# Merging score visits across batch borders in an attention plus MLP kernel

## The chip, the cores and the metric

The kernel runs on one core of one Trainium2 chip. The metric is the device time of one execution in microseconds. Executions are compared by their medians, and ratios are the mean time of one kernel's fast runs over that of the other's of the same rounds, so not quite the ratio of the medians quoted beside them.

## The reference

```python
# B, H, S, Nb, D = 8, 8, 576, 16, 64;  d_model 512, d_ff 2048
k_all = concat([beacon_k, k], axis=2);  v_all = concat([beacon_v, v], axis=2)
scores = q @ k_all.T / sqrt(D), causal over the S keys, free over the Nb beacon keys
a = softmax(scores);  attn = a @ v_all
x = attn.transpose(0, 2, 1, 3).reshape(B * S, H * D)        # 4608 x 512
out = relu(x @ w_in) ** 2 @ w_out
```

## The kernel before

The kernel does not issue its work in program order. It builds a list of operations, each with engines, an assumed duration, a priority and what it needs. A small list scheduler (`Order.run`) plays them against its own clock and emits each engine's instructions in the order that falls out. One added or removed operation therefore shifts the order of everything behind it, and no line of a diff shows that.

The four pairs of heads of a batch give 4 x 1664 = 6656 score columns, that is 13 pieces of 512. The scores contract over 64 rows, so TensorE runs them on half-height tiles, two heads side by side, while all its other work in the stretch that matters here uses the full array. Pieces are therefore gathered in visits of two or three:

```python
PLAN = ((2,2,3,3,3),(2,2,3,3,3),(2,3,3,3,2),(2,3,3,3,2),(2,3,3,3,2),(2,3,3,3,2),(2,3,3,3,2))
...
def add_batch(b):
    ...
    for size in PLAN[b - 1]:
        pos = HP * b + 512.0 * n / PW
        runs = [(0,), (1, 2)] if size == 3 else [tuple(range(size))]
        for k, run in enumerate(runs):
            ...
            qk = add(f"qk{b}.{n + run[0]}", "PE", ..., emit,
                     take=None if k else ("strip", "strip", min(size, 2)),   # two-bank strips, 2 exist
                     gate=None if k else gate_at(pos - SHIFT))               # paced by MLP progress
            if k == 0:
                qk.wide = [None] if size == 3 else []                        # a third piece: 2 of 4 single banks
```

After a visit ScalarE exponentiates each piece (L632 for a strip, L674 for one head of a piece in single banks), VectorE masks it (L715, L719), and TensorE multiplies it with v (L741). The MLP (L904, then L942) fills TensorE in between. The queue of SyncE holds loads, the DMA transposes of q and k (L407) and of the attention output (L791, into `xT`), and the stores.

The softmax here doesn't subtract the row's maximum and nothing guards it: scores larger than these inputs give would overflow.

Of the kernel before, what the change touches and what calls it, by code (L numbers as in the profile page):

```python
# [11 lines left out]
AF = mybir.ActivationFunctionType  # L12
# [35 lines left out]
class Order:  # L48
# [16 lines left out]
    def add(self, *a, **kw):  # L65
        op = Op(*a, **kw)
        op.need = [d for d in op.need if d is not None]
        self.ops.append(op)
        return op
# [134 lines left out]
def kernel(  # L204
# [11 lines left out]
    nc = tc.nc  # L216
    B, H, S, D = q.shape
    Nb = beacon_k.shape[2]
    HP = H // 2
    scale = 1.0 / float(D) ** 0.5  # L220
# [13 lines left out]
    def sb(name, shape, dt):  # L234
        return pool.tile(shape, dt, name=name)

    NSTG, RB = 8, 4
    PW = 1664
# [34 lines left out]
    pt = sb("pt", [128, 2, 8192], BF16)  # L273
# [8 lines left out]
    strips = [psum.tile([128, 2, 512], FP32, name=f"strip{i}") for i in range(2)]  # L282
    ps = [psum.tile([128, 512], FP32, name=f"ps{i}") for i in range(4)]
# [16 lines left out]
    add = order.add  # L300
# [33 lines left out]
    qk_ops = {}  # L334
    av_ops = {}
    load_chain = []

    def t_rows(t):
        return 128 - Nb if t == 0 else rows_of(t)

    def t_start(t):
        return max(0, 128 * t - Nb)
# [207 lines left out]
    class Phase:  # L550
# [3 lines left out]
        def __init__(self, pieces, diag, last, tiles, off):  # L554
            self.pieces, self.diag, self.last, self.tiles, self.off = pieces, diag, last, tiles, off
            self.lo = t_start(tiles[0])
            self.hi = t_start(tiles[-1]) + t_rows(tiles[-1])
# [7 lines left out]
    NPC = HP * PW // 512  # L565
    PIECES = [[] for _ in range(NPC)]
    WHOLE = []
    for pr, segs in enumerate(STREAM):
        off, at = {}, 0
        for c, t0, t1 in segs:  # L570
# [3 lines left out]
            while t0 < t1:  # L574
                n, o = divmod(PW * pr + at, 512)
                w = min(t1 - t0, 512 - o)
                PIECES[n].append((pr, c, t0, t0 + w, o))
                t0, at = t0 + w, at + w
# [31 lines left out]
    def gate_at(pos):  # L610
        return lambda o: o.progress >= mlp_chunk_us * (LEAD + PACE * (pos - HP))

    def deps_of(b, pr, part):
        if b >= NPE:
            return trans[b, "k"] + trans[b, "q"]
        parts = range(part + 1) if b == pr == 0 else [len(parts_of[b]) - 1]
        return [bk_ev[b]] + [trans_part[b, n, pr, x] for n in parts for x in "kq"]

    def emit_scores(b, mms, st):
        for pr, c, t0, t1, at in mms:  # L620
            for hj in range(2):
                hp = slice(64 * hj, 64 * hj + 64)
                nc.tensor.matmul(  # L623
                    st[hj][:, at:at + t1 - t0],
                    kT[b % 2][hp, pr, 128 * c:128 * c + 128],
                    qT[b % 2][hp, pr, t0:t1],
                    start=True, stop=True,
                )

    def add_exp(name, qk, s, at, width, prio, done):  # L630
        def emit(e):
            nc.scalar.activation(pt[:, :, at:at + width], strips[qk.slots[s]][:, :, 0:width],  # L632
                                 AF.Exp, bias=0.0, scale=scale)

        return add(name, "ACT", 0.18 + 2 * width / 1200.0, emit, prio=prio, deps=[done], give=(qk, s))

    exps_of = {}
    SHIFT = 0.25
    PLAN = ((2,2,3,3,3),(2,2,3,3,3),(2,3,3,3,2),(2,3,3,3,2),(2,3,3,3,2),(2,3,3,3,2),(2,3,3,3,2))
    FREE = 2  # L640
    last_qk = []

    def add_batch(b):
        for pr in range(HP):
            p = HP * b + pr
            qk_ops[p], av_ops[p], exps_of[p] = [], [], []
        n = 0
        for size in PLAN[b - 1]:
            pos = HP * b + 512.0 * n / PW
            box = {}  # L650
            runs = [(0,), (1, 2)] if size == 3 else [tuple(range(size))]
            for k, run in enumerate(runs):
                def emit(e, run=run, n=n, box=box, size=size):
                    for s in run:
                        if size == 3 and s == 0:
                            emit_scores(b, PIECES[n], [ps[x] for x in box["qk"].wide])
                        else:
                            st = strips[box["qk"].slots[s - (size == 3)]]
                            emit_scores(b, PIECES[n + s], [st[:, 0, :], st[:, 1, :]])

                qk = add(f"qk{b}.{n + run[0]}", "PE", 0.2 / len(runs) + 512 * len(run) / 2400.0, emit,
                         prio=-1.0e6 if k else 100.0 * pos - 1000.0, behind=[qk] if k else last_qk[-1:] if size == 3 or b > FREE else [],
                         take=None if k else ("strip", "strip", min(size, 2)), gate=None if k else gate_at(pos - SHIFT))
                last_qk.append(qk)
                if k == 0:
                    qk.wide = [None] if size == 3 else []
                    box["qk"] = qk
                for s in run:
                    at, prio = 512 * (n + s), 1.0e-2 * (pos + 0.1 * s) - 30.0
                    if size == 3 and s == 0:  # L670
                        es = []
                        for hj in range(2):
                            def emit_half(e, hj=hj, at=at, qk=qk):
                                nc.scalar.activation(pt[:, hj, at:at + 512], ps[qk.wide[hj]], AF.Exp, bias=0.0, scale=scale)  # L674

                            es.append(add(f"exp{b}.{n}.{hj}", "ACT", 0.18 + 512 / 1200.0, emit_half, prio=prio + 1.0e-4 * hj, deps=[qk],
                                          give=(qk, hj - 2)))
                    else:
                        es = [add_exp(f"exp{b}.{n + s}", box["qk"], s - (size == 3), at, 512, prio, qk)]
                    for pr in sorted({mm[0] for mm in PIECES[n + s]}):  # L680
                        p = HP * b + pr
                        for o in deps_of(b, pr, 0) + av_ops[p - HP]:
                            if o not in box["qk"].need:
                                box["qk"].need.append(o)
                        qk_ops[p].append(qk)
                        exps_of[p] += es
            n += size
        assert n == NPC
        for pr in range(HP):
            add_phase(b, pr, HP * b + pr, 0, WHOLE[pr][0], 100.0 * (HP * b + pr), exps_of[HP * b + pr])  # L690

# [290 lines left out]
    for b in range(B):  # L982
# [8 lines left out]
        for n, (x, c) in enumerate(([] if b < NPE else nat) + [("v", c) for c in range(NT)]):  # L991
            behind, sync = [], []
            if x == "v" and b == 0:
                pass
            elif x == "v" and b == 1 and c == 0:
                behind = [strided[1, 0, HP - 1, "q"]]
            elif b == 2 and n == 0:
                sync = [w_ops["out", 2]]
            elif b >= NPE and x == "v" and c == 0:
                for y in "qk":  # L1000
                    add_trans(b, y, lp - 5.0)
                behind = trans[b, "q"] + trans[b, "k"]
# [7 lines left out]
        if b == 0:  # L1010
            for pr in range(HP):
                add_pair(b, pr)
        else:
            add_batch(b)
# [63 lines left out]
```

## Time and profile before

| | before |
|---|---|
| time, median of 3 | 338.86 us (338.78 to 339.68) |
| span of the profiled execution | 336.1 us, of a run that took 337.79 us |
| TensorE busy | 98% |
| VectorE, ScalarE, GpSimd busy | 50%, 57%, 27% |
| score visits in batches 4 to 7 | 20 |

TensorE is the bound, and a busy share cannot say how much of it is work. Throughout, the times are read from one start to the next: a matmul's listed length overlaps its neighbour, its start does not. Where a start comes later than the columns of the previous matmul explain, at 2.4 columns per ns plus some 2.5 ns, TensorE was switching or waiting. The other thing to know is that some matmul records are lost: the page before counts 3158 matmuls where the program has 3201 (its 3201 weight loads are all listed). A hole of 0.21 to 0.22 us beside 512-column matmuls is such a record and no wait.

### The profile page before, as it was taken

What the parts mean: (1) busy time and instruction counts of PE and PEld (TensorE: products, weight loads), DVE (VectorE), ACT (ScalarE), POOL (GpSimd) and SP (SyncE); (2) the same over time, 40 slices, a digit from 0 to 9 for tenths busy, and PEclk for the clock granted to TensorE, in tenths of its full rate; (3) what the DMA queues carried; (4) which work ended last, traced back from release to release, by engine and by line L of the source; (5) the groups of instructions that cost most, each with busy time, mean ns of one, the idle gap of its engine ahead of it and who ended that gap; (6) DMA issues with size and microseconds to landing.
All of it is one profiled execution on the core that took longest, in us unless ns stands there. A gap on an engine that the chain in (4) does not pass through costs nothing.

```text
span 336.1 us, 7810 instructions
## 1 busy us (share of the span) xinstructions
PE 329.0 (98%) x3158; PEld 189.0 (56%) x3201; DVE 168.4 (50%) x393; ACT 191.3 (57%) x289; POOL 90.9 (27%) x143
## 2 busy tenths in 40 slices
PE   8999999999999999999999999999999999999996
PEld 7577766445564554555458845554555544444444
DVE  4896995058556971477155823674247302301400
ACT  3877865376468736575747674676457216515621
POOL 9684805126306413150334042403000000000000
PEclk9999999999999999999999999999999999999999
DMA  7999999999999997899899989996210231011003
GB/s 139 226 205 219 205 194 213 213 235 212 160 241 224 195 197 137 220 242 182 143 230 226 199 154 177 216 238 126 72 62 2 46 90 62 0 64 62 0 3 125
DMA packets 143955, 51.74 MB, mean 154 GB/s; under 512 B 130702, under 2 KB 138798, under 8 KB 143918
## 3 DMA queue, kind: packets, MB, share of 16 engines
q1 hardware_dynamic: 135375, 42.19, 60.9%
q0 software_dynamic: 7904, 8.69, 15.0%
q8 instruction: 25, 0.41, 0.5%
q10 hardware_dynamic: 639, 0.36, 0.4%
q14 instruction: 12, 0.10, 0.1%
HBM read 37.22 MB, written 9.44 MB: 139 GB/s over the span
## 4 chain that ended last, share of the span: by engine, by line
PE 94%; POOL 2%; DMA 2%; issue 1%; ACT 0%; POOLq 0%; ACTq 0%
PE ps L904 37%; PE ps L942 36%; PE ps L741 9%; PE strip L623 6%; PE ps L623 2%; DMA qk_area<-in_k_dram 2%; PE ps L808 1%; PE ps L487 1%; PE ps L854 1%; POOL qk_area L452 1%; PE ps L296 1%; POOL stg L372 1%; POOL tri L312 0%; ACT osb L326 0%; POOL stg L371 0%
## 5 line engine op out<-in xcount | busy, mean ns | idle before, releaser
L904 PE MATMUL ps<-xT,w_in 128*128 128x512 bf16 (+3 forms) x686 | 132.1, 339 | 0.8
L942 PE MATMUL ps<-w_out,g 128*128 128x512 bf16 x535 | 127.0, 379 | 1.7 <-issue 0.5
L904 PEld LDWEIGHTS <-w_in 128*128 128x128 bf16 x704 | 65.5, 98 | 51.0 <-issue 0.7
L920 ACT ACTIVATE g<-ps 128x512 bf16<-128x512 f32 (+2 forms) x112 | 63.9, 570 | 41.9 <-PE ps L904 40.7
L632 ACT ACTIVATE pt<-strip 128x1024 bf16<-128x1024 f32 (+3 forms) x86 | 81.5, 1004 | 9.0 <-PE strip L623 8.8
L929 DVE TENSOR_TENSOR g<-g 128x1024 bf16<-128x1024 bf16 (+2 forms) x80 | 52.5, 666 | 65.8 <-ACT g L920 64.8
L942 PEld LDWEIGHTS <-g 128*128 128x128 bf16 x560 | 51.6, 98 | 56.5 <-issue 1.5
L328 POOL CAST qk_area<-stg 128x512 bf16<-128x512 f32 (+2 forms) x60 | 40.3, 675 | 65.5 <-DMA stg<-in_k_dram 39.9
L326 ACT COPY osb<-ps 128x512 f32<-128x512 f32 (+2 forms) x34 | 19.3, 571 | 64.6 <-PE ps L942 50.9
L741 PEld LDWEIGHTS <-pt 128*128 128x128 bf16 (+1 forms) x960 | 36.4, 98 | 11.7 <-DVE pt L715 0.8
L328 POOL CAST vb<-stg 128x512 bf16<-128x512 f32 (+1 forms) x38 | 24.4, 651 | 68.5 <-DMA stg<-in_v_dram 66.2
L741 PE MATMUL ps<-vb,pt 128*128 128x65 bf16 (+1 forms) x960 | 39.5, 194 | 0.0
L715 DVE TENSOR_TENSOR pt<-pt,tri 128x512 bf16<-128x512 bf16 x64 | 28.7, 457 | 17.9 <-ACT pt L674 11.3
L922 DVE TENSOR_SCALAR g<-ps 128x512 bf16<-128x512 f32 (+2 forms) x48 | 27.3, 586 | 13.5 <-PE ps L904 11.8
L760 DVE TENSOR_TENSOR xn<-ps,rcp 128x320 bf16<-128x320 f32 (+2 forms) x64 | 31.5, 492 | 2.5 <-DVE rcp L758 0.2
L674 ACT ACTIVATE pt<-ps 128x512 bf16<-128x512 f32 x42 | 22.8, 597 | 15.4 <-PE ps L623 13.1
L758 DVE RECIPROCAL rcp<-ps 128x5 f32<-128x5 f32 (+2 forms) x64 | 12.2, 190 | 33.0 <-PE ps L741 30.0
L623 PEld LDWEIGHTS <-kT 64*128 64x128 bf16 x596 | 19.8, 94 | 15.2 <-issue 13.3
L623 PE MATMUL strip<-qT,kT 64*128 64x208 bf16 (+13 forms) x474 | 27.0, 239 | 0.0
L328 DVE COPY osb<-ps 128x512 f32<-128x512 f32 (+1 forms) x4 | 2.4, 592 | 21.3 <-PE ps L854 11.7
L296 PE MATMUL ps<-g 128*128 128x128 bf16 (+1 forms) x87 | 11.0, 281 | 1.1 <-DVE warm L303 1.1
L372 POOL DMA_DIRECT2D stg<-in_v_dram x10 | 8.6, 866 | 4.5 <-DMA w_in<-in_moe_w_in_dram 3.0
(43 smaller groups left out, 98.2 us busy)
## 6 DMA issues: line engine op xcount, KB each, us to landing
out_dram<-osb SPq DMA_DIRECT2D x17, 512.0 KB, 3.5
stg<-in_q_dram SPq DMA_DIRECT2D x24, 256.0 KB, 5.0
stg<-in_k_dram SPq DMA_DIRECT2D x18, 256.0 KB, 5.5
stg<-in_v_dram SPq DMA_DIRECT2D x18, 256.0 KB, 5.2
w_in<-in_moe_w_in_dram POOLq DMA_DIRECT2D x4, 512.0 KB, 8.3
w_out<-in_moe_w_out_dram POOLq DMA_DIRECT2D x4, 512.0 KB, 11.2
stg<-in_v_dram POOLq DMA_DIRECT2D x6, 256.0 KB, 7.9
stg<-in_k_dram SPq DMA_DIRECT2D x6, 224.0 KB, 3.7
```

The source lines that it names most:

```text
L328: eng[e].tensor_copy(dst, src)
L623: nc.tensor.matmul(st[hj][:, at:at + t1 - t0], kT[b % 2][hp, pr, 128 * c:128 * c + 128], qT[b % 2][hp, pr, t0:t1], start=True, stop=True,)
L632: nc.scalar.activation(pt[:, :, at:at + width], strips[qk.slots[s]][:, :, 0:width], AF.Exp, bias=0.0, scale=scale)
L674: nc.scalar.activation(pt[:, hj, at:at + 512], ps[qk.wide[hj]], AF.Exp, bias=0.0, scale=scale)
L715: nc.vector.tensor_tensor(out=d, in0=d, in1=tri[:, m0:m0 + m, :][:, None].to_broadcast([128, 2, m, 128]), op=ALU.min)
L741: nc.tensor.matmul(a[:, at + (t - tl[0]) * (D + 1):at + (t - tl[0] + 1) * (D + 1)], P[0:rr, hj, o:o + 128], vb[b % 2][0:rr, c, 2 * pr + hj ...
L760: nc.vector.tensor_tensor(out=xn[b % 2].rearrange("p t (h d) -> p h t d", d=D)[:, h0:h0 + nh, tl[0]:tl[0] + nt], in0=a[:, :, :, 0:D], in1= ...
L904: nc.tensor.matmul(h[:, lo - spans[0][0]:hi - spans[0][0]], w_in_sb[:, mc, ft * 128:(ft + 1) * 128], xT[:, mc, lo % RING:lo % RING + hi - lo],
L920: nc.scalar.activation(dst, h, AF.Relu, bias=0.0, scale=1.0)
L922: nc.vector.tensor_scalar(out=dst, in0=h, scalar1=0.0, scalar2=None, op0=ALU.max)
L929: nc.vector.tensor_tensor(out=d, in0=d, in1=d, op=ALU.mult)
L942: nc.tensor.matmul(o, G[:, fc, ts * 128:(ts + 1) * 128], w_out_sb[:, fc, :], start=(fc == 0), stop=(fc == NFT - 1))
```

## The change

The intent is fewer visits. A batch of 13 pieces needs five visits of at most three; four batches together have 52 pieces, which fit into 18 visits where four times five are 20. The plan becomes one list over all batches, and a visit may take its last pieces from the next batch.

```diff
-    PLAN = ((2,2,3,3,3),(2,2,3,3,3),(2,3,3,3,2),(2,3,3,3,2),(2,3,3,3,2),(2,3,3,3,2),(2,3,3,3,2))
+    sizes = list((2,2,3,3,3, 2,2,3,3,3, 2,3,3,3,2, 3,3,3,3,3,3,3,3,3,3,3,3,3,3,3,3,2,2))
+    class Visit:                     # holds its ops and (batch, piece) parts; emits scores of both batches
+        ...
+        for n in range(NPC):
+            if not opened:
+                opened.append(Visit(b, n, sizes.pop(0)))
+            opened[0].add(b, n)
+            if len(opened[0].parts) == opened[0].size:
+                opened.clear()
-        for size in PLAN[b - 1]:
-            ...                      # the same, visit by visit within one batch
```

The title given to the change also names zeroing of batch 0 on VectorE. No line of the diff does that.

More of the change, by code (lines that the diff above doesn't have):

```diff
@@ L638, with __init__, emit, banks @@
     SHIFT = 0.25
-    PLAN = ((2,2,3,3,3),(2,2,3,3,3),(2,3,3,3,2),(2,3,3,3,2),(2,3,3,3,2),(2,3,3,3,2),(2,3,3,3,2))
     FREE = 2
-    last_qk = []
+    sizes = list((2,2,3,3,3, 2,2,3,3,3, 2,3,3,3,2, 3,3,3,3,3,3,3,3,3,3,3,3,3,3,3,3,2,2))
+    assert sum(sizes) == NPC * (B - 1)
+    last_qk, opened = [], []
+    class Visit:
+        def __init__(self, b, n, size):
+            pos = HP * b + 512.0 * n / PW
+            self.size, self.parts, self.ops = size, [], []
+            for k, run in enumerate([(0,), (1, 2)] if size == 3 else [tuple(range(size))]):
+                def emit(e, run=run):
+                    for s in run:
+                        bb, m = self.parts[s]
+                        emit_scores(bb, PIECES[m], self.banks(s))
+                self.ops.append(add(
+                    f"qk{b}.{n + run[0]}", "PE", (0.1 if size == 3 else 0.2) + 512 * len(run) / 2400.0, emit,
+                    prio=-1.0e6 if k else 100.0 * pos - 1000.0,
+                    behind=self.ops[-1:] if k else last_qk[-1:] if size == 3 or b > FREE else [],
+                    take=None if k else ("strip", "strip", min(size, 2)), gate=None if k else gate_at(pos - SHIFT)))
+            self.ops[0].wide = [None] if size == 3 else []
+            last_qk.append(self.ops[-1])
+        def banks(self, s):
+            first = self.ops[0]
+            if self.size == 3 and s == 0:
+                return [ps[x] for x in first.wide]
+            st = strips[first.slots[s - (self.size == 3)]]
+            return [st[:, 0, :], st[:, 1, :]]
+        def add(self, b, n):
+            s = len(self.parts)
+            self.parts.append((b, n))
+            first, op = self.ops[0], self.ops[-1 if s else 0]
+            at, prio = 512 * n, 1.0e-2 * (HP * b + 512.0 * n / PW) - 30.0
+            if self.size == 3 and s == 0:
+                es = []
+                for hj in range(2):
+                    def emit_half(e, hj=hj):
+                        nc.scalar.activation(pt[:, hj, at:at + 512], ps[first.wide[hj]], AF.Exp, bias=0.0, scale=scale)
+                    es.append(add(f"exp{b}.{n}.{hj}", "ACT", 0.18 + 512 / 1200.0, emit_half, prio=prio + 1.0e-4 * hj,
+                                  deps=[op], give=(first, hj - 2)))
+            else:
+                es = [add_exp(f"exp{b}.{n}", first, s - (self.size == 3), at, 512, prio, op)]
+            for pr in sorted({mm[0] for mm in PIECES[n]}):
+                p = HP * b + pr
+                for o in deps_of(b, pr, 0) + av_ops[p - HP]:
+                    if o not in first.need:
+                        first.need.append(o)
+                qk_ops[p].append(op)
+                exps_of[p] += es
@@ L646, in add_batch @@
             qk_ops[p], av_ops[p], exps_of[p] = [], [], []
-        n = 0
-        for size in PLAN[b - 1]:
-            pos = HP * b + 512.0 * n / PW
-            box = {}
-            runs = [(0,), (1, 2)] if size == 3 else [tuple(range(size))]
-            for k, run in enumerate(runs):
-                def emit(e, run=run, n=n, box=box, size=size):
-                    for s in run:
-                        if size == 3 and s == 0:
-                            emit_scores(b, PIECES[n], [ps[x] for x in box["qk"].wide])
-                        else:
-                            st = strips[box["qk"].slots[s - (size == 3)]]
-                            emit_scores(b, PIECES[n + s], [st[:, 0, :], st[:, 1, :]])
-                qk = add(f"qk{b}.{n + run[0]}", "PE", 0.2 / len(runs) + 512 * len(run) / 2400.0, emit,
-                         prio=-1.0e6 if k else 100.0 * pos - 1000.0, behind=[qk] if k else last_qk[-1:] if size == 3 or b > FREE else [],
-                         take=None if k else ("strip", "strip", min(size, 2)), gate=None if k else gate_at(pos - SHIFT))
-                last_qk.append(qk)
-                if k == 0:
-                    qk.wide = [None] if size == 3 else []
-                    box["qk"] = qk
-                for s in run:
-                    at, prio = 512 * (n + s), 1.0e-2 * (pos + 0.1 * s) - 30.0
-                    if size == 3 and s == 0:
-                        es = []
-                        for hj in range(2):
-                            def emit_half(e, hj=hj, at=at, qk=qk):
-                                nc.scalar.activation(pt[:, hj, at:at + 512], ps[qk.wide[hj]], AF.Exp, bias=0.0, scale=scale)
-                            es.append(add(f"exp{b}.{n}.{hj}", "ACT", 0.18 + 512 / 1200.0, emit_half, prio=prio + 1.0e-4 * hj, deps=[qk],
-                                          give=(qk, hj - 2)))
-                    else:
-                        es = [add_exp(f"exp{b}.{n + s}", box["qk"], s - (size == 3), at, 512, prio, qk)]
-                    for pr in sorted({mm[0] for mm in PIECES[n + s]}):
-                        p = HP * b + pr
-                        for o in deps_of(b, pr, 0) + av_ops[p - HP]:
-                            if o not in box["qk"].need:
-                                box["qk"].need.append(o)
-                        qk_ops[p].append(qk)
-                        exps_of[p] += es
-            n += size
@@ L688, in add_batch @@
-        assert n == NPC
+        for n in range(NPC):
[4 more added lines that the diff above has]
+                opened.clear()
         for pr in range(HP):
```

## The prediction

> **What bounds the kernel now.** I read the page first: its busy line, its slices, its chain.
>
> ```profile
> PE 329.0 (98%) x3158; PEld 189.0 (56%) x3201; DVE 168.4 (50%) x393; ACT 191.3 (57%) x289; POOL 90.9 (27%) x143
> ...
> PE   8999999999999999999999999999999999999996
> ...
> PE 94%; POOL 2%; DMA 2%; issue 1%; ACT 0%; POOLq 0%; ACTq 0%
> ```
>
> TensorE is busy 98% of 336.1 us in all but the first and last slice, and 94% of the chain that ended last is TensorE. Busy alone proves little, because matmuls are pipelined and their durations overlap, so I went to the stretches and then to starts. The stretches, columns being us, then busy time and count of PE, PEld, DVE, ACT and POOL, clock, DMA share and GB/s:
>
> ```profile
> 30.00:148.00 118.00, 116.76 (x1253) 67.62 (x1267) 73.86 (x173) 72.90 (x107) 43.72 (x68) 1.00 1.05 207
> 148.00:263.00 115.00, 113.78 (x1122) 66.36 (x1138) 60.25 (x139) 70.69 (x105) 24.84 (x38) 1.00 0.79 154
> 263.00:336.10 73.10, 69.70 (x351) 33.37 (x354) 12.83 (x21) 26.90 (x47) 0.00 (x0) 1.00 0.16 52
> ```
>
> The change acts in the last part of batch 4 and on to batch 7, nearly all in the middle row. There VectorE has 52% and ScalarE 61% of the time, at full clock; TensorE is the bound. After 263 us there is only the MLP, whose work the change leaves alone. The timeline of TensorE around two score visits (L623), columns being start, length, engine, line, operation, count:
>
> ```profile
> 178.66 0.40 PE L623 MATMUL ps<-qT,kT 64*128 64x144 bf16 x6
> 178.90 0.61 PE L623 MATMUL strip<-qT,kT 64*128 64x176 bf16 x14
> 179.44 5.41 PE L904 MATMUL ps<-xT,w_in 128*128 128x256 bf16 x48
> ...
> 184.69 0.61 PE L741 MATMUL ps<-vb,pt 128*128 128x65 bf16 x15
> 185.14 1.04 PE L904 MATMUL ps<-xT,w_in 128*128 128x256 bf16 x8
> 186.11 0.61 PE L623 MATMUL strip<-qT,kT 64*128 64x272 bf16 x12
> 186.66 0.63 PE L741 MATMUL ps<-vb,pt 128*128 128x65 bf16 x15
> 187.13 3.66 PE L904 MATMUL ps<-xT,w_in 128*128 128x256 bf16 x32
> 190.62 0.62 PE L741 MATMUL ps<-vb,pt 128*128 128x65 bf16 x15
> ```
>
> The reader is to use starts, not lengths. Thirty-two L904 matmuls run from 187.13 to 190.62: 0.109 us each. Eight of them from 185.14 should give 0.87, but the visit starts only after 0.97: going in costs 0.10. A visit of two pieces takes 186.11 to 186.66, 0.55; one of three takes 178.66 to 179.44, 0.78. The third piece is worth 0.23, so two are 0.46 and 0.09 of the 0.55 is fixed: coming out. **A visit has a fixed price of 0.19 us**, whatever its size. A pass over all starts between 148 and 263 us agrees: in 0.098, out 0.095, every visit. Beyond these the pass finds holes of 0.21 to 0.22 us, which are lost records (one 512-column matmul each), and one true wait of TensorE, 0.27 us near 173:
>
> ```profile
> 171.80 1.27 DVE L715 TENSOR_TENSOR pt<-pt,tri 128x512 bf16<-128x512 bf16 x2
> ...
> 172.68 0.86 POOL L328 CAST qk_area<-stg 128x512 bf16<-128x512 f32 x1 [0.35 <-DMA stg<-in_q_dram]
> ...
> 172.98 0.64 DVE L719 TENSOR_TENSOR pt<-pt,tri 80x160 bf16<-80x160 bf16 x1
> ```
>
> The last mask took 0.64 us, where the median of its 32 is 0.23, beside casts on GpSimd, and the attention matmul behind it was late.
>
> **What the Trainium skill says.** "TensorEngine Tiling (Array Packing)", Key Properties: "Changing tiling mode (not just tile) drains the TensorE". The scores use half-height tiles (64*128), all else 128*128; the trace agrees, at 0.10 in and 0.09 out. "TensorE: Matmul & The Clock Gate", Back-to-back issue gap: the isolated warm gap is N/2.4 + 2.5 ns; the trace agrees (256 columns: 109.2 ns worked out, 109 measured), so the PE time of a sequence of instructions can be added up. "SBUF — State Buffer", on the shared port pair: VectorE work with two SBUF inputs and GpSimd's reads shut each other out for a whole instruction. The 0.64 us mask is what that would look like, and such delays are what a schedule of fixed durations cannot foresee.
>
> **The change part by part.**
> Zeroing on VectorE: the title names it, but no line of the diff does it. The padding is already zeroed by VectorE before, GpSimd's order is the same in both programs, and TensorE's first 3019 of 6404 instructions are identical. Worth 0.
> Visits: batches 4 to 7 have 52 pieces of 512 columns. Before, 2+3+3+3+2 per batch, 20 visits. After, sixteen of three and two of two, 18. Matmuls and weight loads stay 6404 in number with the same columns. Removed: 2 x 0.19 = **0.38 us of TensorE time**, on the path, since TensorE has no slack there. That is 0.11% of 338.86.
> ScalarE: a three-piece visit puts its first piece in two single PSUM banks, exponentiated in two halves. Four more such visits: 8 x 597 ns added (L674), 4 x 1032 ns removed (L632), +0.65 us on an engine with some 44 us idle in the stretch. The program order also moves three relus from VectorE to ScalarE and three output copies the other way: about nil. All beside TensorE's work.
> Moved: the order of everything after about 150 us. Laying both programs' TensorE orders end to end with these rates (an estimate from the trace), the last attention matmul of batch 4 comes some 9 us later than before, that of batch 5 some 8 us later, that of batch 7 0.4 us earlier. So the shuffle has closed again before the MLP tail, and what remains is 0.38 less any new wait.
>
> **The rivals.**
> First, the plain sum: TensorE stays full, 338.86 - 0.38 = 338.5. For it: one wait of 0.27 us in 115 us, and that one may even go.
> Second, a PSUM or exponential wait takes the place of the removed switches. Four more visits each hold two more of the four single banks. From the last matmul in a bank to the next write there, the tightest turn round of an MLP bank was 1.72 us of TensorE work; in the new order two are 1.30 and four 1.41. An eviction needs about 0.2 us to start (last L904 matmul done at 186.01, ScalarE began at 186.21) and 0.6 to run, with a signal back about 0.9, so 0.4 us is left if the engine is free at once. Batch 6 now needs all three pieces of a visit before each attention matmul: two halves and two full exponentials are 2 x 0.60 + 2 x 1.03 = 3.26 us, masks of two at 0.43 and one at 0.23 make 1.1, together some 4.7 with signals, and the order leaves 5.3. Batch 4's pair 3 has 3.1 us, but needs only the two halves and the mask, 2.3 and signals. Two or three misses of 0.2 to 0.4 us would eat the gain: 338.7 to 339.2.
> Third, a visit across a border needs the next batch's transposed q and k earlier. The transposes of k were issued at 151.50, 185.26 and 218.14 us and land 5.6 us later by the median. Batch 5 is wanted at about 159.8, as before; batch 7 at about 226.8, later than before; batch 6 at about 192.0 instead of 193.4, with 190.9 landed: 1.1 us of slack where 2.5 was. And batch 4's transposes into xT go out from about 167 instead of 159.91, behind six loads and a store, and are wanted by 175.9. At 1.27 us for each of the first three and 2.5 to land, about 173.5 is met. If that queue slips by 2 us, TensorE waits about 1 us: 339.5.
>
> **Range and chances.** I take the gain of 0.38 and 0.15 us for new waits, less the old one that may go: 338.86 - 0.38 + 0.15, about **338.6 us**. The three runs of before lie between 338.78 and 339.68 and the profiled one took 337.79, so run-to-run spread is larger than the effect. Range **337.8 to 339.6**. A change of 2% would be 6.8 us, eighteen times the whole saving or seven slips of the third kind: faster 0.003, same 0.99, slower 0.007.
>
> **What would show each step.** L623 should lie in two visits fewer after 125 us, each still at 0.10 and 0.09 around it; a different price would sink the first step. The long MLP stretch that begins behind the last attention matmul, at 263.54 us before, should begin 0.1 to 0.4 us earlier. Exponentials: 82 full and 50 halves, where 86 and 42 stood. TensorE holes other than lost records should stay under 0.5 us after 148 us. Holes before L741 with masks or exponentials behind them, or before L904 or L942 with evictions, speak for the second rival; a hole before L623 near 192, or before L904 near 176 us ended by a DMA, for the third. I am wrong if the kernel comes out more than 0.8 us off, which would need a wait I have not placed.

## The result

| | before | after |
|---|---|---|
| median, first rounds | 338.82 us (338.76 to 339.68, 4 runs) | 338.19 us (337.92 to 339.06, 4 runs) |
| ratio | | 0.998, interval 0.9955 to 1.0005 |
| profiled execution, span | 336.1 us | 337.3 us (a run of 339.06 us) |

338.19 us lies in the range of 337.8 to 339.6 and 0.4 us from the point. Faster by 0.63 us at the medians, within 2%, and the interval includes no change. The profiled execution of the changed kernel is longer than that of the kernel before, so the spans of the two profiles cannot be compared as they stand. In the changed kernel the same work has other line numbers: L754 is the old L741 (times v), L917 and L955 are the MLP's L904 and L942, L678 is L674, and the masks are L728 and L732. The page of the changed kernel (busy line, then the shares of the chain, then groups):

```profile
PE 331.6 (98%) x3201; PEld 189.5 (56%) x3201; DVE 169.9 (50%) x393; ACT 191.7 (57%) x293; POOL 89.6 (27%) x143
...
PE 79%; DMA 13%; POOL 5%; SPq 1%; issue 1%; ACT 0%; POOLq 0%
...
L955 PE MATMUL ps<-w_out,g 128*128 128x512 bf16 x560 | 131.1, 379 | 0.8 <-DMA w_out<-in_moe_w_out_dram 0.8
...
L632 ACT ACTIVATE pt<-strip 128x1024 bf16<-128x1024 f32 (+3 forms) x82 | 77.8, 1004 | 7.1 <-PE strip L623 6.9
...
L678 ACT ACTIVATE pt<-ps 128x512 bf16<-128x512 f32 x50 | 27.1, 597 | 16.5 <-PE ps L623 15.8
```

Busy time of TensorE went up by 2.6 us, and that is no added work: this trace lost no record, the one before lost 43, and both programs have 3201 matmuls. The exponentials are 82 and 50, as worked out. The chain is now 13% DMA, because TensorE waited once for the last quarter of `w_out` near 50 us and once for batch 7's transposed k near 229 us, and the chain follows these transfers back, the first of them to the start. Here is the first place in the timeline (start, length, engine, line, operation, count, then idle before and what ended it):

```profile
49.38 0.61 PE L754 MATMUL ps<-vb,pt 128*128 128x65 bf16 x15
50.82 1.02 PE L955 MATMUL ps<-w_out,g 128*128 128x512 bf16 x4 [0.83 <-DMA w_out<-in_moe_w_out_dram]
```

Fifteen L754 matmuls take 0.46 us elsewhere, here 1.44: a wait of about 1.0 us near 50 us, far ahead of the change. The instructions of TensorE are the same in both programs up to the first visit of batch 4, which starts at 126.78 us in the trace before and at 128.49 us in this one. The two starts (the visit of three of the changed kernel is listed in two lines):

```profile
126.78 0.61 PE L623 MATMUL strip<-qT,kT 64*128 64x112 bf16 x10
...
128.49 0.39 PE L623 MATMUL ps<-qT,kT 64*128 64x112 bf16 x6
128.72 0.60 PE L623 MATMUL strip<-qT,kT 64*128 64x144 bf16 x10
```

So 1.7 us were lost on identical instructions before the change acts.

From that visit on, the picture turns round. The profile of the changed kernel around the same MLP work as in the prediction:

```profile
180.64 5.41 PE L917 MATMUL ps<-xT,w_in 128*128 128x256 bf16 x48
185.89 0.61 PE L754 MATMUL ps<-vb,pt 128*128 128x65 bf16 x15
186.35 1.04 PE L917 MATMUL ps<-xT,w_in 128*128 128x256 bf16 x8
187.22 0.62 PE L754 MATMUL ps<-vb,pt 128*128 128x65 bf16 x15
```

Where the visit of two stood between the eight MLP matmuls and the attention matmuls, nothing stands now: eight take 0.87 us to the next start and not 0.97. The way to count this exactly is to take the stretch from the start of the first visit of batch 4 to the start of the last matmul and to take out the true waits (holes that are neither a switch nor a lost record):

| trace | first visit of batch 4 | from there to the last matmul | waits in it | net | visits in it |
|---|---|---|---|---|---|
| before | 126.78 | 206.07 | 0.27 | 205.80 | 20 |
| after | 128.49 | 205.61 | 0.26 | 205.35 | 18 |

The net falls by 0.45 us. From the start of the last matmul both spans have 3.24 us left.

### The profile page after: what moved, and what is told of

Same layout as the page of the kernel before. It is cut to its first block, busy times and chain, and to the rows that moved or that the text cites. A ratio compares the mean times of both kernels' runs of the same rounds, so it can differ in the third digit from the quotient of the medians.

```text
span 337.3 us, 7857 instructions
## 1 busy us (share of the span) xinstructions
PE 331.6 (98%) x3201; PEld 189.5 (56%) x3201; DVE 169.9 (50%) x393; ACT 191.7 (57%) x293; POOL 89.6 (27%) x143
## 4 chain that ended last, share of the span: by engine, by line
PE 79%; DMA 13%; POOL 5%; SPq 1%; issue 1%; ACT 0%; POOLq 0%
PE ps L955 35%; PE ps L917 30%; PE ps L754 7%; DMA w_out<-in_moe_w_out_dram 4%; PE strip L623 4%; DMA qk_area<-in_q_dram 4%; PE ps L623 2%; DMA stg<-in_v_dram 2%; POOL qk_area L452 2%; SPq L407 1%; DMA kT<-qk_area 1%; DMA stg<-in_k_dram 1%; PE ps L867 1%; POOL stg L372 1%; PE ps L821 1%
## 5 line engine op out<-in xcount | busy, mean ns | idle before, releaser
L917 PE MATMUL ps<-xT,w_in 128*128 128x512 bf16 (+3 forms) x704 | 133.3, 340 | 0.0
L955 PE MATMUL ps<-w_out,g 128*128 128x512 bf16 x560 | 131.1, 379 | 0.8 <-DMA w_out<-in_moe_w_out_dram 0.8
L917 PEld LDWEIGHTS <-w_in 128*128 128x128 bf16 x704 | 65.7, 98 | 51.2 <-issue 1.1
L933 ACT ACTIVATE g<-ps 128x512 bf16<-128x512 f32 (+2 forms) x115 | 65.7, 571 | 42.9 <-PE ps L917 41.9
L942 DVE TENSOR_TENSOR g<-g 128x1024 bf16<-128x1024 bf16 (+2 forms) x80 | 51.9, 657 | 69.9 <-ACT g L933 68.9
L955 PEld LDWEIGHTS <-g 128*128 128x128 bf16 x560 | 51.5, 98 | 56.5 <-issue 2.0
L632 ACT ACTIVATE pt<-strip 128x1024 bf16<-128x1024 f32 (+3 forms) x82 | 77.8, 1004 | 7.1 <-PE strip L623 6.9
L326 ACT COPY osb<-ps 128x512 f32<-128x512 f32 (+2 forms) x31 | 17.6, 570 | 65.4 <-PE ps L955 52.6
L754 PEld LDWEIGHTS <-pt 128*128 128x128 bf16 (+1 forms) x960 | 36.3, 98 | 11.4 <-issue 0.5
L754 PE MATMUL ps<-vb,pt 128*128 128x65 bf16 (+1 forms) x960 | 39.3, 194 | 0.0
L678 ACT ACTIVATE pt<-ps 128x512 bf16<-128x512 f32 x50 | 27.1, 597 | 16.5 <-PE ps L623 15.8
L728 DVE TENSOR_TENSOR pt<-pt,tri 128x512 bf16<-128x512 bf16 x64 | 29.4, 468 | 6.7 <-ACT pt L678 4.3
L935 DVE TENSOR_SCALAR g<-ps 128x512 bf16<-128x512 f32 (+2 forms) x45 | 25.6, 580 | 13.2 <-PE ps L917 12.5
L623 PE MATMUL strip<-qT,kT 64*128 64x112 bf16 (+13 forms) x452 | 25.7, 238 | 0.0
L328 DVE COPY osb<-ps 128x512 f32<-128x512 f32 (+1 forms) x7 | 4.4, 635 | 31.3 <-PE ps L955 19.4
L623 PE MATMUL ps<-qT,kT 64*128 64x208 bf16 (+15 forms) x144 | 9.9, 240 | 0.2 <-DMA kT<-qk_area 0.2
```

The costliest lines, as they stand in the source:

```text
L328: eng[e].tensor_copy(dst, src)
L623: nc.tensor.matmul(st[hj][:, at:at + t1 - t0], kT[b % 2][hp, pr, 128 * c:128 * c + 128], qT[b % 2][hp, pr, t0:t1], start=True, stop=True,)
L632: nc.scalar.activation(pt[:, :, at:at + width], strips[qk.slots[s]][:, :, 0:width], AF.Exp, bias=0.0, scale=scale)
L678: nc.scalar.activation(pt[:, hj, at:at + 512], ps[first.wide[hj]], AF.Exp, bias=0.0, scale=scale)
L728: nc.vector.tensor_tensor(out=d, in0=d, in1=tri[:, m0:m0 + m, :][:, None].to_broadcast([128, 2, m, 128]), op=ALU.min)
L754: nc.tensor.matmul(a[:, at + (t - tl[0]) * (D + 1):at + (t - tl[0] + 1) * (D + 1)], P[0:rr, hj, o:o + 128], vb[b % 2][0:rr, c, 2 * pr + hj ...
```

## The experiments

All edits are against the changed kernel. The table collects what the traces of all kernels gave, in the same way; the text after it says what follows. "Mean" is over fast runs, with the mean of the kernel before in the same rounds.

| kernel | visits from batch 4 | first visit of batch 4 | waits behind it | net | mean, before's mean |
|---|---|---|---|---|---|
| again | 18 | 127.10 | 0.46 | 205.36 | 338.35, 338.27 |
| again2 | 18 | 127.28 | 0.10 | 205.36 | 337.97, 338.24 |
| cross20 | 20 | 127.56 | 0.00 | 205.78 | 337.89, 338.27 |
| half19 | 19 | 128.97 | 0.00 | 205.57 | 338.20, 338.27 |
| twos26 | 26 | 127.49 | 0.00 | 207.05 | 339.98, 338.44 |
| full_first | 18 | 128.20 | 1.07 | 205.46 | 339.45, 338.44 |
| feed7 | 18 | 128.04 | 2.38 | 205.36 | 339.32, 338.24 |
| feed7b | 18 | 126.48 | 2.17 | 205.35 | one run, 338.96 |

### again and again2: the changed kernel twice more

No edit.

> The changed kernel once more, five rounds beside the kernel before. Theory (only the two removed visits pay, 0.19 us each): 0.3 to 0.5 us faster than before by the medians, ratio near 0.9988; from the first visit of batch 4 to the last matmul 205.6 us as in the first trace of it (before: 206.07). Rival (a new order that loses other waits): faster by 0.6 us or more, as the first four runs said. Start-up theory: the stretch up to the first visit of batch 4 differs between executions by up to 2 us in either kernel, with the hole before the first L955 matmul near 50 us as its largest single part.

> The changed kernel a third time, beside the next three on one chip. Net of waits, 205.35 us from the first visit of batch 4 to the last matmul, as in both earlier traces of it. Feeding theory: batch 7's transpose of k is issued at 221 us or later, and its first visit, near 228 us, waits for it by 0 to 1 us, differently in each execution.

Ratios were 1.0002 (0.9984 to 1.0019) and 0.9994 (0.9971 to 1.0017), medians of fast runs 338.18 against 338.16 and 337.74 against 338.18. The net is 205.36 in both, so what the change does to TensorE's work repeats to 0.01 us. What it does to the time does not: the three comparisons of medians give -0.63, +0.02 and -0.44 us. The wait of again is at 207 us. The timeline there, of VectorE, of GpSimd and of TensorE:

```profile
205.53 2.08 DVE L728 TENSOR_TENSOR pt<-pt,tri 128x512 bf16<-128x512 bf16 x2
207.54 0.23 DVE L732 TENSOR_TENSOR pt<-pt,tri 80x160 bf16<-80x160 bf16 x1
```

```profile
205.42 1.92 POOL L328 CAST qk_area<-stg 128x512 bf16<-128x512 f32 x3 [1.67 <-DMA stg<-in_k_dram]
```

```profile
207.67 0.63 PE L754 MATMUL ps<-vb,pt 128*128 128x65 bf16 x15 [0.29 <-DVE pt L728]
```

Two masks, some 0.85 us together at their median, took 2.08 beside three casts of GpSimd, and the attention matmul of batch 6's pair 1 was late. It is the kind of wait that the kernel before had near 173 us. "SBUF — State Buffer" of the Trainium skill, on the shared port pair, has VectorE work with two SBUF inputs and GpSimd's reads shut each other out; the masks that took more than twice their median beside casts agree, but that the port is the cause was not tested. When the casts come depends on when loads land, which differs from one execution to the next.

### cross20 and half19: crossing without saving, and half the saving

```diff
-    sizes = [..., 3,3,3,3,3,3,3,3,3,3,3,3,3,3,3,3,2,2]             # batches 4 to 7
+    sizes = [..., 3,3,3,3,2,3,3,3,3, 2,2,3,3,3, 2,2,2,2,2,3]       # cross20
+    sizes = [..., 3,3,3,3,3,3,3,3,2, 2,3,3,3,2, 2,3,3,3,2]         # half19
```

> Batches 4 to 7 cross a border once and are shuffled in order, but keep 20 visits (12 of three, 8 of two). Theory (count of visits): time of the kernel before, within 0.15 us. Rival (the new order itself, or the wait near 173 us that goes with the old order): as fast as the changed kernel, 0.4 us or more below before.

> Batches 4 and 5 share 9 visits, batches 6 and 7 keep five each: 19 visits. Theory: half the gain, 0.2 us below before, and 0.19 us less from the first visit of batch 4 to the last matmul, plus or minus any wait. Rival (order): no proportion.

Net times are 205.78 for 20 visits, with a new order and a crossing, and 205.57 for 19. Before is 205.80 for 20, after 205.35 for 18. So the saving in net time goes with the count of visits and neither with the crossing nor with the order. The clock alone would have misled: cross20 came out at a ratio of 0.9988 (0.9975 to 1.0001), as fast as the best of the others, against what the count theory expected; its trace has no wait behind 126 us. half19's ratio was 0.9997 (0.9979 to 1.0016). Effects of 0.2 to 0.4 us are below what five rounds resolve here.

### twos26: eight visits more

```diff
+    sizes = [..., 2 x 26]                                          # batches 4 to 7
```

> Batches 4 to 7 in 26 visits of two pieces, eight more than in the changed kernel. Theory (price per visit): from the first visit of batch 4 to the last matmul, waits taken out, 205.35 + 8 x 0.22 = 207.1 us; the whole 1.5 to 2.0 us slower than the changed kernel, near 340. Rival (single PSUM banks held by three-piece visits are what matters): no more waits on banks, so no slower than before.

Net 207.05, expected 207.1: (207.05 - 205.35) / 8 = 0.21 us per visit. The whole is slower too, 339.94 us, ratio 1.0046 (1.0023 to 1.007). Two-piece visits use no single banks, and the kernel is slower all the same, so the rival falls. Its trace has no wait at all behind 126 us, but one execution does not show that banks are the reason.

### full_inside and full_first: the switch of tiling alone

```diff
                         bb, m = self.parts[s]
+                        if s == 1:                                  # full_first: s == 0
+                            nc.tensor.matmul(self.banks(s)[0][:, 0:8], ident, ident[:, 0:8], start=True, stop=True)
                         emit_scores(bb, PIECES[m], self.banks(s))
```

The 8 columns are overwritten by the scores, so the result stays right.

> The changed kernel with one full-array matmul of 8 columns put between the first and second piece of each of the 33 visits: two more switches of the array's tiling per visit. Theory (the switch of tiling is the price): 33 x (0.19 + about 0.03 for the matmul itself), some 7 us more TensorE time, time near 345. Rival (the price lies in the neighbours of a visit, in their weights or banks, not in the switch): as full_first.

> Control for full_inside: the same 33 matmuls of 8 columns, but before each visit's first piece, beside full-array work, so no switch is added. Both theories: 33 x about 0.03, some 1 us more than the changed kernel, time near 339.3.

Taken from the first visit of batch 1 to the last matmul, net, the changed kernel has 298.40 us, full_first 298.64 and full_inside 305.61. The matmul itself costs (298.64 - 298.40) / 33 = 0.007 us, less than the 0.03 that I had allowed. In the middle of a visit it costs (305.61 - 298.40) / 33 = 0.218. The difference, **0.21 us, is one way out of the half-height tiles and back**. Times agree: 345.18 us, ratio 1.0203, against 339.59 for the control, ratio 1.0029. (The control's time is near the 339.3 expected, but for another reason: in its one trace the small matmuls added 0.24 us, and waits did the rest.) The timeline of one visit in full_inside:

```profile
169.99 0.39 PE L623 MATMUL ps<-qT,kT 64*128 64x96 bf16 x6
170.32 0.18 PE L653 MATMUL strip<-ident 128*128 128x8 bf16 x1
170.43 0.62 PE L623 MATMUL strip<-qT,kT 64*128 64x128 bf16 x12
170.98 0.64 PE L756 MATMUL ps<-vb,pt 128*128 128x65 bf16 x15
```

A three-piece visit takes 0.78 us without the small matmul and 170.98 - 169.99 = 0.99 with it. The control showed something else as well, which the next experiment takes up:

```profile
228.52 0.17 PE L653 MATMUL ps<-ident 128*128 128x8 bf16 x1
229.62 0.40 PE L623 MATMUL ps<-qT,kT 64*128 64x112 bf16 x6 [0.94 <-DMA kT<-qk_area]
```

The first visit of batch 7 stood still for 1.0 us until its transposed k had landed.

### feed7 and feed7b: batch 7's k earlier

```diff
                 v_loads[b].append(load_chain[-1])
+            load_chain[-1].prio = -60.0 if (b, x != "v") == (7, True) else load_chain[-1].prio
```

The queue of SyncE before and after, as the timelines have it around batch 7's transposes:

```profile
213.65 3.77 SPq L407 DMA_TRANSPOSE qT<-qk_area  x1
...
218.14 3.91 SPq L407 DMA_TRANSPOSE kT<-qk_area  x1
```

```profile
213.17 4.99 SPq L407 DMA_TRANSPOSE qT<-qk_area  x1
218.20 1.21 SPq L372 DMA_DIRECT2D stg<-in_k_dram  x2
...
224.03 2.99 SPq L407 DMA_TRANSPOSE kT<-qk_area  x1
```

In the changed kernel two loads of k go out behind the transpose of q and have to land and be cast first, so the transpose of k is issued at 221.00 to 224.03 us in its three traces, where it was 218.14. The visit waited 0.26 us in the first trace and not in the other two. The edit moves two loads ahead of five transposes in the queue of SyncE; TensorE's order changes only around batch 7's first visit. The wait of 0.26 us in the first trace of the changed kernel reads:

```profile
229.01 0.39 PE L623 MATMUL ps<-qT,kT 64*128 64x112 bf16 x6 [0.19 <-DMA kT<-qk_area]
```

The transposed k had landed at 228.97 us.

> The changed kernel, but the last two loads of k of batch 7 go out before batch 5's transposes into xT, not after them and batch 7's transpose of q. Feeding theory: the transpose of k follows that of q at once, near 217 us, as in the kernel before, no hole before the first visit of batch 7, net time unchanged at 205.35, and a mean 0.1 to 0.4 us below the changed kernel. Rival (the waits there are chance from elsewhere): a hole of 0.2 us or more there in some execution, same mean.

> The same kernel as feed7 for a second trace: again no hole before the first visit of batch 7, and the transpose of k near 217 us.

No hole stands before batch 7's visit in either trace, but two of the three traces of the unedited kernel have none either, so this does not show what made the transpose late. What is shown is what the visit waited for: the releaser named in two traces (the first one and the control's) is the transpose of k. The rest of the expectation failed: the transpose of k went out at 221.87 and 219.83 us, not 217. Counted from the first visit of batch 4 that is 93.8 and 93.4 us, against 95.5, 93.9 and 94.0 without the edit, so it hardly came earlier. The kernel was no faster (median 338.91, ratio 1.0032, 1.0 to 1.0064; 1.0020 without the run at a clock of 0.994). The net is the same 205.36 and 205.35. A new wait has appeared, here in feed7b:

```profile
208.38 1.03 PE L955 MATMUL ps<-w_out,g 128*128 128x512 bf16 x4
211.41 1.02 PE L917 MATMUL ps<-xT,w_in 128*128 128x512 bf16 x4 [2.00 <-DMA xT<-xn]
```

With those loads ahead of them, batch 5's transposes into `xT` began at 209.06 and 207.22 us instead of some 202 to 205.5, and the MLP waited 1.4 and 2.2 us for them. One in-order queue feeds both, and loads that went ahead in it for one consumer made another wait.

### all31, late32f and sync3: attempts at a faster kernel

```diff
+    sizes = [2,2, 3 x 29]                                           # all31: 31 visits
+    sizes = [2,2,3,3,3, 2,2,3,3,3, 3 x 21, 2]                        # late32f: 32 visits, with feed7's edit
-                sync = [w_ops["out", 2]]
+                sync = [w_ops["out", 3]]                             # sync3: plan of the changed kernel
```

> The same merging from batch 1 on: two visits of two, then 29 of three, 31 visits in all where the changed kernel has 33. Theory: another 0.38 us below the changed kernel, about 0.8 below before, if the earlier batches have no new wait. Rival (feeding): batches 2 and 3 get their transposed q and k or their free PSUM banks later than the visits ask, TensorE waits 0.5 us or more and the kernel is no faster than the changed one.

> Feed7 with batch 3's border merged too: 32 visits in all, 17 from the first visit behind 126 us if it falls there. Count theory: 0.21 us less net TensorE time over the whole than feed7 (298.18 from the first visit of batch 1), and as much faster if no wait is added. Rival (feeding): batch 4 or 5 now waits, as with all31, and the time is that of feed7 or worse.

> The changed kernel with the loads of batch 2 held back until the fourth quarter of w_out has landed, not the third; from there the order of instructions is a new one. Start-up theory (a late fourth quarter, sharing the DMA engines with batch 2's loads, is the largest part of the spread between executions): no hole before L955 near 50 us, and a mean 0.3 to 0.5 us below the changed kernel with a smaller spread. Rival: the quarter is late for other reasons, the hole stays in some executions and the time is the same.

All three are slower: 340.29 us (ratio 1.0079), 342.09 (1.0107) and 342.15 (1.0105). Without their runs at clocks of 0.995 and less the ratios are 1.0063, 1.0071 and 1.0097, so the order stands. The count theory holds in their net from the first visit of batch 1: 298.86 for the 35 visits of before, 298.40 for 33, 298.19 for 32, 298.04 for 31. But all31 waits 1.8 us for a mask near 101 us and 1.0 for a normalised output near 105 that TensorE itself transposes; late32f waits 2.6 us at 142 and 0.9 at 178. The waits for TensorE by their releasers, late32f behind 126 us:

```profile
PE ps L917 <- DMA xT<-xn: 2.4, 1, 2.4
PE ps L754 <- DVE pt L728: 0.8, 1, 0.8
```

sync3's one trace has no hole near 50 us, as expected of a later start of batch 2's loads, but one execution is no proof, since the changed kernel's second trace has none there either. Its new order waits 1.2 and 0.9 us for `xT` at 176 and 210 us, and the start-up gain could not be seen in the time. No version beat both kernels clearly.

### What makes the executions differ

Nine traces have the same TensorE order up to the first visit of batch 4: before, after and all in the table but full_first. In these nine the visit starts anywhere from 126.48 to 128.97 us, a spread of 2.5 us on identical instructions. The wait for the last quarter of `w_out` near 50 us is a part of it: 0.06, 0.99, 0.00, 0.53, 0.12, 1.06, 0.45, 0.00 and 0.16 us in before, after, again, again2, cross20, half19, twos26, feed7 and feed7b. The moment of the first MLP matmul is another, 23.16 to 24.93 us. Together they are nearly all of it: the start of the visit, less both, is 103.1 to 103.4 us in all nine. Against this stands a saving of 0.45 us. Why the loads land at different times was not tested.

## Why the prediction was right

The point of 338.6 us came out 0.4 us off, but that is no proof: the kernel before, at 338.82 us, lies in the predicted range too, so no effect at all would have passed. What tests the mechanism is the net time.

- **TensorE is full and its work adds up.** Right: net times repeat to 0.02 us among kernels of equal count (205.80 and 205.78; 205.35 and 205.36). The new order worked out end to end held as well: from the first visit of batch 4, the last attention matmul of batch 4 comes 9.1 us later than before, that of batch 5 7.5 later, that of batch 7 0.46 earlier. One reading was too broad: "all else 128*128" is true of the stretch, but the first batches' transposes on TensorE (L487) are listed as 96*64.
- **A visit has a fixed price of 0.19 us.** Right in kind and a little small: 0.21 to 0.23 us, from 20, 19, 18 and 26 visits, and 0.21 from the added switches. The 0.098 in and 0.095 out (counted over the columns alone; 0.096 and 0.093 over columns plus 2.5 ns) are measured again in every trace. The first starts inside a visit are some 0.01 us late too, which my reading of the ends left out; the rest of the difference, about 0.01, I cannot place.
- **0.38 us of saving on the path.** 0.45 us by the trace, for the reason just named.
- **ScalarE's added 0.65 us is beside the work.** Right: no hole in TensorE's stream behind 126 us ends with ScalarE alone.
- **The plain sum as first rival** describes the net. The second rival appeared in the form of its exponentials and masks: the wait of 0.46 us in again is at batch 6's pair 1, one of the pairs for which I had counted 4.7 us needed and 5.3 left; two masks that ran 1.2 us over their median used up that 0.6. No hole was found behind the tighter PSUM banks.
- **The third rival** came at the wrong place, and this is the step that failed: I kept batch 7's transpose of k at its old 218.14 us and called batch 7 safe. The new queue order issues it at 221 to 224 us, and batch 7's visit waited 0.26 us (1.0 in the control kernel). Batch 6, for which I feared it, never waited, though its margin was thinner than worked out: I took 190.9 us from the median landing time, but the trace before has that transpose landing at 191.81, 0.2 us ahead of the 192.0 wanted and not 1.1. In the three traces it landed 0.3, 1.0 and 1.1 us ahead of the visit. The `xT` of batch 4, which I called met, was in time in the three traces of the changed kernel; feed7, whose TensorE order is the same up to there, waited 0.7 us for it near 177 us, so that margin is thin too.
- **0.15 us for new waits less old ones.** The three traces of the changed kernel have 0.26, 0.46 and 0.10 us, mean 0.27; the one trace before has 0.27. So the waits roughly cancel, and 338.86 - 0.45 would be the better centre; three comparisons of medians, -0.63, +0.02 and -0.44, average -0.35 and do not contradict it.
- **The MLP stretch behind the last attention matmul should begin 0.1 to 0.4 us earlier than 263.54.** This test was badly chosen. The 263.54 was the start of the last L904 matmul ahead of it; the first L942 behind it starts at 263.76 us before and at 265.01, 263.82 and 263.65 in the three traces, because it carries the start-up spread. A test must count from an anchor behind the spread.

## What to carry to other kernels

When the expected effect is smaller than the spread of executions, don't ask the clock: anchor a stretch of the trace on an instruction ahead of the change, take the waits and lost records out, and compare what is left. When an engine is full, a switch of its mode has a price that can be counted, here 0.21 us for each way out and back. A scheduler that shuffles everything behind one edit also shuffles the in-order DMA queue, so look up the new issue time of every transfer that a bound engine waits for, and don't carry the old one over.

## What the Trainium skill lacked or had wrong

- "TensorEngine Tiling (Array Packing)", Key Properties, says that a change of tiling mode drains TensorE but gives no price. Here it is 0.098 us going in and 0.095 coming out, counted over the columns alone, and 0.21 us for a round trip measured by added switches.
- "TensorE: Matmul & The Clock Gate", Back-to-back issue gap, gives about 131 ns per matmul as the sustained rate at 512 columns with weight loads, and calls N/2.4 + 2.5 an isolated figure that over-counts. Here the isolated formula holds in sustained streams of weight load and matmul pairs: 48 matmuls of 256 columns from 180.64 to 185.89 us are 109 ns each, where the formula gives 109.2, and four of 512 columns from 48.51 to 49.38 us are 217 ns each, where it gives 215.8. For 65 columns, 15 take 0.46 us, some 30 ns each.
- "Perfetto Trace Analysis" does not say how a lost matmul record looks in a profile: some traces here lack 42 or 43 of 3201, each a hole of 0.21 to 0.22 us beside 512-column matmuls that looks like a wait.
